# Weighing parts spaced by dense matmuls, a smaller memset and some value copies on VectorE, in an attention and token-MLP kernel

## The chip, the cores and the metric

The kernel runs on one core of a Trainium2 chip. Its time is device microseconds of one execution. A core has five engines that work side by side from their own instruction queues: TensorE (PE; its weight loads are listed as PEld), VectorE (DVE), ScalarE (ACT), GpSimd (POOL) and SyncE (SP, which issues the transfers here). An engine waits where an instruction needs another engine's result or a buffer that another engine still reads.

## What is computed

Two branches share one normalized input of 2048 tokens by 1024 features. Branch A is attention in 4 segments of 512 tokens, 32 heads of 32 columns, with a memory carried from segment to segment. Branch B is an MLP across tokens. Their sum and the input are the output.

```python
x  = A_x
xn = _layernorm(x)
return x + _A_ref(xn, wq, wk, wv, wo, beta) + _B_ref(xn, w1, b1, w2, b2)

# branch A, for each segment s, per head
logits = q_s @ k_s.T * scale + mask          # causal
a_dot  = softmax(logits) @ v_s
a_mem  = (phi(q_s) @ M) / (phi(q_s) @ z + 1e-06)
o      = g * a_mem + (1 - g) * a_dot
M, z   = M + phi(k_s).T @ v_s, z + sum(phi(k_s))
# at the end: o @ wo

# branch B
y = gelu(layernorm(xn).T @ w1 + b1) @ w2 + b2   # over tokens, transposed back
```

Here phi(t) is t + 1 for positive t and exp(t) otherwise.

## The kernel before

The program is written as one stream; a small framework class (`FW`) puts each operation on an engine and adds the waits that its reads and writes need. `FW.mm` (line 198) issues every matmul, so all matmuls have line 198 in the profile and are told apart by their tiles. PSUM has 8 banks of 128x512 fp32; the framework orders readers and writers by bank.

**First half.** Normalization, then branch B as two chains of block products (`products`, with seven products in place of eight for each 2x2 block of a pair of chunks). A result bank is added into fp32 `part` tiles on DVE (`add_bank`, line 690). While the last pair of the second chain runs, `before_attention` (from line 995) lays out the attention's tiles in memory that is no longer used, loads `wv` and `wo`, computes the gates (`gates`, lines 545 to 559, small DVE operations, the last of them a 128x32 copy at line 558), and sets the three value tiles `vA` to 1.0 on POOL (line 1024). A value tile is 128 x 4 x 16 x 33: 4 chunks of 128 tokens, 16 heads, 32 value columns and one column of ones. With that column, the product of probabilities and values also gives the softmax's row sum, and the memory product also gives z.

**Second half: `attention` (line 1350).** Work goes by units, u = 0 to 31: segment s = u // 8, and 4 heads at a time. A unit's own steps are these:

- `logits(u, step)`: scores of four heads in row tiles into banks 0 to 3, then one exp on ACT over 128x2048 into `pT` (line 1212), then the causal mask on the diagonal blocks on POOL (line 1216). Step 0 is key block 0; step 1 is key blocks 1 and 3; step 2, in even units alone, is key block 2 of two units. The three steps share banks 0 to 3, so each waits for the exp of the one before.
- `weigh(u - 1, part)`: the probabilities of the unit before, times `vA` (matmuls of 33 columns), and from segment 1 on phi(q) times the memory (132 columns). Parts 0 and 2 use bank 4, part 1 uses bank 5. Each part is copied by DVE into `ost` (line 1263). Part 2 also makes the memory update, which DVE adds into `MZ32` and writes masked to `MZbf` (lines 1269 to 1274).
- `combine(u - 1)`: reciprocals, gate, products and a sum on DVE, into `o_s` (lines 1284 to 1321); `phi_q`, `phi_k` (lines 1080 and 1082); two transposes by DMA; for some units one chunk of the next segment's input (`xn_scale`, line 986, and a transposing DMA). These steps are put on a list, `side`.

**Dense work.** Between these steps stand the projections, as jobs of 8 matmuls of 512 columns: `wo_job` for an output of an earlier segment, `v_job` for a chunk of values, `q_job` and `k_job` for the unit after next, in this order. `unit_jobs(u)` collects them: 24 matmuls in segment 0 and in some late units, 32 in most others. Jobs take turns on banks 6 and 7, so the job after next needs the bank that this one's result is copied from. The last matmul of a job is followed by its copy: ACT for q (line 1103) and, before the change, for every v (line 1139), DVE for k (line 1112) and for the output addition (`fin`, line 1154). `v_job(m, c)` makes chunk c of half-segment m; units 4(m-1) to 4(m-1)+3 hold the four chunks of m, and m = 0 stands ahead of unit 0.

`dense(n)` issues n of these matmuls. While `side` is not empty, it pops one of its steps after every third matmul. So the order within a unit is fixed by `cut(total, shares)`, which divides the unit's dense matmuls among the places between the steps:

- even units, shares (5, 1, 3, 15, 8) of 32: logits 0, 5, weigh 0 and 1, 1, weigh 2, 3, logits 1, 15, logits 2, 8;
- odd units, shares (7, 4, 1, 4, 16): 7, logits 0, 4, weigh 0 and 1, 1, weigh 2, 4, logits 1, 16.

With 24 matmuls the numbers are scaled and rounded: 4, 0, 3, 11, 6 and 5, 3, 1, 3, 12.

`tail` (line 1420) weighs the last unit and finishes the last 512 tokens' output.

Of the kernel before, what the change touches and what calls it, by code (L numbers as in the profile page):

```python
# [6 lines left out]
ACT = mybir.ActivationFunctionType  # L7
# [8 lines left out]
D_HEAD = 32  # L16
# [368 lines left out]
class _Kernel:  # L385
# [609 lines left out]
    def before_attention(self, p):  # L995
        fw = self.fw
        if p == 1:
            self.walk = _Walk(self.mem, self.G_AT, self.B_AT)
            for k in range(2):
                self.wq_ring.ensure(k)  # L1000
                self.wk_ring.ensure(k)
            self.gates()
        take = self.walk.take

        def many(name, n, shape, dtype, parts=1):
            tiles, res = [], []
            for k in range(n):
                t, r = take(f"{name}{k}", shape, dtype, parts)
                tiles.append(t)
                res.append(r if parts > 1 else r[0])  # L1010
            return tiles, res

        if p == 6:
            self.wv, self.R_wv = take("wv", [P, N_DCH, D_MODEL], BF16, 2)
            for bv in range(2):
                fw.dma(self.wv[:, :, bv * 512:(bv + 1) * 512],
                       self.A_wv[:, bv * 512:(bv + 1) * 512].rearrange("(dc p) j -> p dc j", p=P), writes=[self.R_wv[bv]])
            self.vA, self.R_vA = many("vA", 2, [P, 4, 16, VW], BF16, 4)
        elif p == 5:
            a, b = many("vA_", 1, [P, 4, 16, VW], BF16, 4)  # L1020
            self.vA += a
            self.R_vA += b
            for k in range(3):
                fw.op("pool", lambda e: e.memset(self.vA[k][:], 1.0), writes=self.R_vA[k])
            self.qT, self.R_qT = many("qT", 3, [P, SEG_L], BF16)
            self.kT, self.R_kT = many("kT", 3, [P, SEG_L], BF16)
            self.etmp, self.R_etmp = many("etmp", 4, [P, SEG_L], BF16)
            self.mtmp, self.R_mtmp = many("mtmp", 2, [P, SEG_L], BF16)
        elif p == 7:
            self.pqT, self.R_pqT = many("pqT", 3, [P, SEG_L], BF16)  # L1030
            self.pk, self.R_pk = many("pk", 2, [P, 4, P], BF16)
            self.ost, self.R_ost = many("ost", 2, [P, 32, VW], BF16, 3)
            self.o_s, self.R_os = many("o_s", 2, [P, 4, P], BF16)
            self.prod, (self.R_prod,) = take("prod", [P, 32, D_HEAD], BF16)
        elif p == 2:
            self.wo, (self.R_wo,) = take("wo", [P, N_GRP, D_MODEL], BF16)
            fw.dma(self.wo[:], self.A_wo.rearrange("(jc p) j -> p jc j", p=P), writes=[self.R_wo])
        elif p == 3:
            self.pT = take("pT", [P, 2, 4, PT_COLS], BF16)[0]
            base = self.mem.live.pop()  # L1040
            self.R_pu = [[Res(f"pu{b}{k}", dict(base[2][0].r)) for k in range(4)] for b in range(2)]
            self.R_pd = [[Res(f"pd{b}{k}", dict(base[2][0].r)) for k in range(4)] for b in range(2)]
            self.mem.live.append((base[0], base[1], [r for rows in self.R_pu + self.R_pd for r in rows]))
            self.xnT[1], self.R_xnT[1] = take("xnT1", [P, N_DCH, SEG_L], BF16, 4)
            w = _Walk(self.mem, self.B_AT, self.B_AT + self.STG_AT)
            self.MZ32, self.R_MZ32 = w.take("MZ32", [P, N_GRP, GW], F32, N_GRP)
            self.MZbf, self.R_MZbf = w.take("MZbf", [P, N_GRP, GW], BF16, N_GRP)
            self.diag, (self.R_diag,) = w.take("diag", [P, 4, VW], F32)
            self.oT, self.R_oT = [], []
            for k in range(2):  # L1050
                t, r = w.take(f"oT{k}", [P, N_GRP, SEG_L], BF16, N_GRP)
                self.oT.append(t)
                self.R_oT.append(r)
            w = _Walk(self.mem, self.B_AT + 88320, self.B_AT + 96512)
            self.fin, self.R_fin = [], []
            for k in range(4):
                t, r = w.take(f"fin{k}", [P, D_MODEL], BF16, 2)
                self.fin.append(t)
                self.R_fin.append(r)
            fw.op("dve", lambda e: e.memset(self.diag[:], 0.0), writes=[self.R_diag])  # L1060
            for r in range(4):
                fw.op("dve", lambda e: e.memset(self.diag[32 * r:32 * r + 32, r, :], 1.0),
                      reads=[self.R_diag], writes=[self.R_diag])
# [67 lines left out]
    def v_job(self, m, c):  # L1131
        s, bv, i = m // 2, m % 2, m % 3

        def mm(b, dc):
            self.fw.mm(self.bank(b), self.xnT[s % 2][:, dc, c * P:(c + 1) * P], self.wv[:, dc, bv * 512:(bv + 1) * 512],
                       start=(dc == 0), stop=(dc == 7))

        def end(b):
            self.fw.op("act", lambda e: e.activation(self.vA[i][:, c, :, 0:D_HEAD],  # L1139
                                                     self.bank(b).rearrange("p (h d) -> p h d", d=D_HEAD), ACT.Copy),  # L1140
                       reads=[self.R_bank[b]], writes=[self.R_vA[i][c]])

        return [0, None, lambda: [self.R_wv[bv], self.R_xnT[s % 2][c]], mm, end]

# [205 lines left out]
    def attention(self):  # L1350
        self.jobs, self.turn = deque(), 0
        self.side, self.since = deque(), 0
        self.exps, self.in_etmp = [], [None] * 4
        self.wo_plan = {}
        for s in range(N_SEG - 1):
            at = [N_GRP * s + 10 + n for n in range(8)] if s < 2 else [27, 28, 29, 30, 30, 31, 31, 31]
            for n, u in enumerate(at):
                self.wo_plan.setdefault(u, []).append((4 * s + n // 2, n % 2))
        self.jobs.extend([self.q_job(0), self.k_job(0)] + [self.v_job(0, c) for c in range(4)])
        self.dense(16)  # L1360
        self.late_exps()
        self.phi_k(0)
        self.k_transpose(0)
        self.jobs.extend([self.q_job(1), self.k_job(1)])
        self.dense(100)
        self.load_fin(0)
        self.load_fin(1)
        for u in range(N_UNIT):
            even = u % 2 == 0
            self.jobs.extend(self.unit_jobs(u))  # L1370
            total = 8 * len(self.jobs) - sum(j[0] for j in self.jobs)
            c = 4 * (u // N_GRP + 1) + u % N_GRP
            xn = u % N_GRP < 4 and c < N_TCH
            if xn:
                self.xn_load(c)
            cuts = self.cut(total, (5, 1, 3, 15, 8) if even else (7, 4, 1, 4, 16))
            if even:
                self.logits(u, 0)
            else:
                self.dense(cuts[0])  # L1380
                self.logits(u, 0)
            if u > 1:
                self.o_transpose_dma(u - 2)
            self.dense(cuts[0] if even else cuts[1])
            if u:
                self.weigh(u - 1, 0)
                self.weigh(u - 1, 1)
            self.dense(cuts[1] if even else cuts[2])
            if u:
                self.weigh(u - 1, 2)  # L1390
                steps = self.combine(u - 1)
                self.side.append(steps.pop(0))
            if N_GRP <= u:
                self.side.append(lambda: self.phi_q(u))
            if u:
                self.side.extend(steps)
            if u + 1 < N_UNIT:
                self.side.append(lambda: (self.phi_k(u + 1), self.k_transpose(u + 1)))
            if xn:
                self.side.append(lambda: (self.xn_scale(c), self.xn_transpose(c)))  # L1400
            self.dense(cuts[2] if even else cuts[3])
            self.logits(u, 1)
            if even:
                self.dense(cuts[3])
                self.logits(u, 2)
            self.dense(100)
            while self.side:
                self.side.popleft()()
        self.tail()
# [83 lines left out]
```

## Time and profile before

| | before |
|---|---|
| median of 3 runs | 671.02 us (670.72 to 673.8) |
| profiled execution | 676.49 us |
| its span in the trace | 674.8 us |
| TensorE busy | 648.7 us, 96% |
| VectorE busy | 424.5 us, 63% |
| ScalarE busy | 279.8 us, 41% |
| GpSimd busy | 148.4 us, 22% |
| mean granted TensorE clock | 0.995 |
| attention | from about 354 us to the end |

The profiled execution took 1.69 us more than its span; this lies before the first and after the last instruction of the trace. A row of the wait table reads: the engine, tile and line that waited, the engine, tile and line that released it, then us in total, the number of times and the longest one. A row of a timeline reads: start, duration, engine, line, operation, output tile <- input tiles, shape, count, and in brackets the idle time before it with what ended it. Times inside the trace count from the start of the span. In segment 0 (about 368 to 435 us) DVE is busy about half of the time and ACT about two thirds to four fifths; from 450 to 600 us DVE is busy over four fifths of the time.

### The profile page before, as it was taken

The numbers are of one execution on the slowest core, as the hardware profiler recorded it, in microseconds if no ns is written. First come the engines' busy times: TensorE is split into PE (matmuls) and PEld (weight loads), VectorE is DVE, ScalarE is ACT, GpSimd is POOL, SyncE is SP. The second block draws the span as 40 slices with busy tenths as digits, with TensorE's granted clock in tenths as the row PEclk, the third lists the DMA queues.
The fourth block names the chain that finished last, engine by engine and source line by source line (L and its number), as shares of the span: only waits on it lengthen the run. The fifth ranks groups of instructions, "written<-read, shape, count | busy, mean of one in ns | idle before, by whom it ended". The sixth has DMA issues, their size and how long they took to land.

```text
span 674.8 us, 11066 instructions
## 1 busy us (share of the span) xinstructions
PE 648.7 (96%) x4568; PEld 302.5 (45%) x4622; DVE 424.5 (63%) x813; ACT 279.8 (41%) x305; POOL 148.4 (22%) x181
## 2 busy tenths in 40 slices
PE   8999999999999999999989999989999999999988
PEld 3444444444444444444434444444444444444444
DVE  6975766656643344433632554578888888776795
ACT  7532322313200000000104777866767666667650
POOL 2500000000022022220430333333233233332340
PEclk9999999999999999999989999999999999999999
DMA  9704232422926755456555784457544774534324
GB/s 302 198 1 125 82 106 63 123 65 63 249 80 171 202 156 151 111 146 171 118 196 150 169 149 96 110 134 149 126 91 107 179 173 103 127 86 79 80 79 133
DMA packets 187243, 87.65 MB, mean 130 GB/s; under 512 B 116025, under 2 KB 174393, under 8 KB 187193
## 3 DMA queue, kind: packets, MB, share of 16 engines
q1 hardware_dynamic: 187048, 86.91, 50.9%
q8 instruction: 36, 0.59, 0.4%
q14 instruction: 15, 0.11, 0.1%
q10 hardware_dynamic: 144, 0.03, 0.0%
HBM read 67.13 MB, written 8.39 MB: 112 GB/s over the span
## 4 chain that ended last, share of the span: by engine, by line
PE 84%; DVE 10%; ACT 3%; issue 2%; DMA 1%; SPq 0%; DVEq 0%
PE ps_all L198 84%; DVE ost L1263 2%; ACT pT L1212 2%; DVE prod L1310 1%; DVE gate L558 1%; DVE mtmp L1080 1%; DMA xin<-in_A_x_dram 1%; DVE pqT L1082 1%; DVE fin L1440 1%; DVE kT L1112 1%; DVE mtmp L1082 1%; ACT vA L1139 0%; DVE fin L1154 0%; DVE srec L1305 0%; DVE o_s L1316 0%
## 5 line engine op out<-in xcount | busy, mean ns | idle before, releaser
L1212 ACT ACTIVATE pT<-ps_all 128x2048 bf16<-128x2048 f32 x80 | 150.1, 1876 | 63.9 <-PE ps_all L198 63.9
L1216 POOL TENSOR_SCALAR_AFFINE_SELECT pT<-pT 128x512 bf16<-128x512 bf16 x128 | 95.4, 762 | 212.4 <-ACT pT L1212 212.4
L690 DVE TENSOR_TENSOR part<-ps_all,part 128x512 f32<-128x512 f32 x76 | 57.3, 754 | 118.8 <-PE ps_all L198 117.9
L926 POOL TENSOR_TENSOR part<-part,stg 128x512 f32<-128x512 f32 x24 | 33.0, 1403 | 266.7 <-DVE part L690 266.7
L695 ACT ACTIVATE part<-ps_all 128x512 f32<-128x512 f32 x20 | 11.9, 597 | 149.0 <-PE ps_all L198 149.0
L742 ACT ACTIVATE g<-part,b1c 128x512 f16<-128x512 f32 x36 | 26.0, 722 | 98.8 <-DVE part L690 98.8
L1263 DVE CAST ost<-ps_all 128x396 bf16<-128x396 f32 (+2 forms) x96 | 42.9, 474 | 37.2 <-PE ps_all L198 37.2
L198 PE MATMUL ps_all<-xnT,wk 128*128 128x512 bf16 x251 | 60.6, 379 | 3.9 <-ACT vA L1139 3.1
L198 PE MATMUL ps_all<-wv,xnT 128*128 128x512 bf16 x238 | 62.9, 382 | 1.2 <-issue 0.8
L198 PE MATMUL ps_all<-wo,oT 128*128 128x512 bf16 (+2 forms) x249 | 59.6, 367 | 2.2 <-DVE fin L1154 0.9
L198 PE MATMUL ps_all<-xnT,wq 128*128 128x512 bf16 x248 | 60.2, 379 | 0.6 <-issue 0.5
L198 PE MATMUL ps_all<-g,sum 128*128 128x512 f16 x224 | 52.7, 388 | 2.6 <-DVE part L690 2.6
L198 PE MATMUL ps_all<-vA,pT 128*128 128x33 bf16 x1280 | 45.4, 178 | 9.0 <-DVE ost L1263 8.8
L198 PEld LDWEIGHTS ps_all<-vA,pT 128*128 128x128 bf16 x1280 | 42.0, 96 | 22.3 <-DVE ost L1263 12.9
L198 PE MATMUL ps_all<-g,w2s 128*128 128x512 f16 x224 | 51.0, 379 | 0.0
L198 PE MATMUL ps_all<-gT,sum 128*128 128x512 f16 x224 | 49.7, 379 | 0.0
L198 PE MATMUL ps_all<-h,sum 128*128 128x512 f16 x192 | 45.2, 379 | 0.0
L198 PE MATMUL ps_all<-h,w1s 128*128 128x512 f16 x192 | 44.9, 379 | 0.0
L198 PE MATMUL ps_all<-hT,sum 128*128 128x512 f16 x192 | 43.6, 379 | 0.0
L1310 DVE TENSOR_TENSOR prod<-ost,srec 128x512 bf16<-128x512 bf16 x48 | 40.2, 837 | 0.9
L1112 DVE CAST kT<-ps_all 128x512 bf16<-128x512 f32 x32 | 22.0, 687 | 26.9 <-PE ps_all L198 26.8
L198 PEld LDWEIGHTS ps_all<-xnT,wk 128*128 128x128 bf16 x256 | 23.4, 98 | 34.3 <-issue 9.0
(98 smaller groups left out, 815.8 us busy)
## 6 DMA issues: line engine op xcount, KB each, us to landing
w2s<-in_B_w_dram SPq DMA_DIRECT2D x8, 1792.0 KB, 8.6
w1s<-in_B_w_dram SPq DMA_DIRECT2D x12, 1024.0 KB, 5.6
wq<-in_A_wq_dram SPq DMA_DIRECT2D x32, 256.0 KB, 3.2
wk<-in_A_wk_dram SPq DMA_DIRECT2D x32, 256.0 KB, 3.5
stg<-in_A_x_dram SPq DMA_DIRECT2D x16, 256.0 KB, 3.0
xs<-in_A_x_dram SPq DMA_DIRECT2D x16, 256.0 KB, 3.6
out_dram<-stg SPq DMA_DIRECT2D x16, 256.0 KB, 3.0
fin<-out_dram SPq DMA_DIRECT2D x16, 256.0 KB, 3.2
```

What stands on the lines that cost most here:

```text
L198: ins = self.nc.tensor.matmul(*args, **kwargs)
L558: fw.op("dve", lambda e: e.tensor_copy(self.gate[:, :, 1, :], gv), reads=[self.R_gcol, self.R_gate], writes=[self.R_gate])
L690: self.fw.op("dve", lambda e: e.tensor_tensor(self.tmp[dst][:], self.bank(b), self.tmp[src][:], op=ALU.add), reads=[self.R_bank[b], self.R ...
L695: self.fw.op("act", lambda e: e.activation(self.tmp[dst][:], self.bank(b), ACT.Copy), reads=[self.R_bank[b]], writes=[self.R_tmp[dst]])
L742: self.fw.op("act", lambda e: e.activation(self.gB[f % 2][half][:, f // 2, :], src, ACT.Gelu_apprx_tanh, bias=self.b1c[:, f:f + 1], scale= ...
L926: fw.op("pool", lambda e: e.tensor_tensor(self.tmp[t][:], self.tmp[t][:], self.stg[k][:, 512 * half:512 * half + 512], op=ALU.add), reads= ...
L1082: fw.op("dve", lambda e: e.scalar_tensor_tensor(dst, src, 1.0, mt[:], op0=ALU.add, op1=ALU.max), reads=[R_src, self.R_mtmp[k]], writes=[R_ ...
L1112: fw.op("dve", lambda e: e.tensor_copy(self.kT[k][:], self.bank(b)), reads=[self.R_bank[b]], writes=[self.R_kT[k]])
L1212: fw.op("act", lambda e: e.activation(dst, src, ACT.Exp, scale=SCALE), reads=self.R_bank[0:4], writes=[R[v % 2][kb] for v, kb, _ in blocks ...
L1216: fw.op("pool", lambda e: e.affine_select(d, d, pattern=[[0, 4], [1, P]], compare_op=ALU.is_ge, fill=0.0, base=0, channel_multiplier=-1), ...
L1263: fw.op("dve", lambda e: e.tensor_copy(dst, src), reads=[self.R_bank[b]], writes=[self.R_ost[o][part]])
L1310: fw.op("dve", lambda e: e.tensor_tensor(self.prod[:, n, :], ost[:, n, 0:D_HEAD], rec[:, n].unsqueeze(2).to_broadcast([P, 16, D_HEAD]), op ...
```

## The change

Three edits. In `before_attention` the memset of each value tile touches the column of ones alone (64 elements a partition in place of 2112). In `v_job`, the copies of half-segments m = 1 and m = 2, which are made in units 0 to 7, go to VectorE; all others stay on ScalarE. In `attention` the cuts have new shares, and the three weighing parts no longer follow one another closely: part 1 has a place of its own, with 2 of 32 dense matmuls on each side, and part 2 is followed by 2 rather than 3 or 4 before logits 1.

With 32 dense matmuls the new orders are:

- even: logits 0, 4, weigh 0, 2, weigh 1, 2, weigh 2, 2, logits 1, 14, logits 2, 8;
- odd: 7, logits 0, 3, weigh 0, 2, weigh 1, 2, weigh 2, 2, logits 1, 16.

With 24: 3, 1, 2, 2, 10, 6 in the dense places of even units, and 5, 3, 1, 1, 2, 12 in those of odd ones.

```diff
@@ before_attention
             for k in range(3):
-                fw.op("pool", lambda e: e.memset(self.vA[k][:], 1.0), writes=self.R_vA[k])
+                fw.op("pool", lambda e: e.memset(self.vA[k][:, :, :, D_HEAD:], 1.0), writes=self.R_vA[k])
@@ v_job
         def end(b):
-            self.fw.op("act", lambda e: e.activation(self.vA[i][:, c, :, 0:D_HEAD],
-                                                     self.bank(b).rearrange("p (h d) -> p h d", d=D_HEAD), ACT.Copy),
-                       reads=[self.R_bank[b]], writes=[self.R_vA[i][c]])
+            dst, src = self.vA[i][:, c, :, 0:D_HEAD], self.bank(b).rearrange("p (h d) -> p h d", d=D_HEAD)
+            if m in (1, 2):
+                self.fw.op("dve", lambda e: e.tensor_copy(dst, src), reads=[self.R_bank[b]], writes=[self.R_vA[i][c]])
+            else:
+                self.fw.op("act", lambda e: e.activation(dst, src, ACT.Copy), reads=[self.R_bank[b]],
+                           writes=[self.R_vA[i][c]])
@@ attention
-            cuts = self.cut(total, (5, 1, 3, 15, 8) if even else (7, 4, 1, 4, 16))
-            if even:
-                self.logits(u, 0)
-            else:
-                self.dense(cuts[0])
-                self.logits(u, 0)
+            cuts = self.cut(total, (0, 4, 2, 2, 2, 14, 8) if even else (7, 3, 2, 2, 2, 16))
+            self.dense(cuts[0])
+            self.logits(u, 0)
             if u > 1:
                 self.o_transpose_dma(u - 2)
-            self.dense(cuts[0] if even else cuts[1])
+            self.dense(cuts[1])
             if u:
                 self.weigh(u - 1, 0)
+            self.dense(cuts[2])
+            if u:
                 self.weigh(u - 1, 1)
-            self.dense(cuts[1] if even else cuts[2])
+            self.dense(cuts[3])
             if u:
                 self.weigh(u - 1, 2)
                 steps = self.combine(u - 1)
...
-            self.dense(cuts[2] if even else cuts[3])
+            self.dense(cuts[4])
             self.logits(u, 1)
             if even:
-                self.dense(cuts[3])
+                self.dense(cuts[5])
                 self.logits(u, 2)
```

## The prediction

> **What bounds the kernel now.** First the shares and the wait table (who waited for whom: total us, times, longest), then the timeline around each wait.
>
> ```profile
> PE 648.7 (96%) x4568; PEld 302.5 (45%) x4622; DVE 424.5 (63%) x813; ACT 279.8 (41%) x305; POOL 148.4 (22%) x181
> ...
> PEld ps_all L198 <- DVE ost L1263: 12.9, 27, 2.1
> ...
> PE ps_all L198 <- DVE ost L1263: 8.8, 24, 1.7
> ...
> PE ps_all L198 <- ACT vA L1139: 3.1, 6, 0.5
> ...
> PE ps_all L198 <- DVE part L690: 2.6, 1, 2.6
> ```
>
> TensorE is the bound: it stands idle 26 of 674.8 us, and each edit aims at one of the last three rows. A matmul's modelled end hides part of a wait, so I price waits from start to start: a 512-column matmul starts 0.216 us after the one before (28 of them, 331.26 to about 337.32), a 33-column one after 0.0256, a 132-column one after 0.055, a logits step takes 0.33. 54 matmul records are missing (4,568 against 4,622 weight loads); most sit right behind a wait, so a 0.40 gap with a matmul of the code missing in it counts as 0.18.
>
> The largest single loss is at the start of the attention (timelines of POOL, DVE and PE, then windows: PE, PEld, DVE, ACT, POOL busy, clock, DMA):
>
> ```profile
> 334.51 5.45 POOL L1024 MEMSET vA<- 128x2112 bf16 x3 [9.93 <-PE ps_all L198]
> ...
> 334.45 5.54 DVE L558 COPY gate<-gcol 128x32 f32<-128x32 f32 x1
> 334.54 5.45 DVE L690 TENSOR_TENSOR part<-ps_all,part 128x512 f32<-128x512 f32 x1
> ...
> 340.07 4.88 PE L198 MATMUL ps_all<-g,sum 128*128 128x512 f16 x14 [2.60 <-DVE part L690]
> ...
> 340.00:342.00 2.00, 1.93 (x5) 0.70 (x6) 0.00 (x0) 0.00 (x0) 0.00 (x0) 0.55 1.07 349
> 342.00:344.00 2.00, 2.00 (x7) 0.76 (x6) 0.00 (x0) 0.00 (x0) 0.00 (x0) 0.60 0.11 33
> ```
>
> A 128x32 copy takes 5.54 us where the like of it at L556 takes 0.18; it ends with the third memset. The sum behind it (L690) is what product 7 waits for. Then TensorE runs at 0.55 to 0.60 of its clock until 344.
>
> Inside the attention, two repeating waits (a unit of segment 0):
>
> ```profile
> 385.09 0.56 PE L198 MATMUL ps_all<-vA,pT 128*128 128x33 bf16 x16 [0.31 <-DVE ost L1263]
> ...
> 389.43 0.59 PE L198 MATMUL ps_all<-xnT,wk 128*128 128x512 bf16 x2 [0.51 <-ACT vA L1139]
> ...
> 386.92 1.88 ACT L1212 ACTIVATE pT<-ps_all 128x2048 bf16<-128x2048 f32 x1 [1.26 <-PE ps_all L198]
> 388.70 0.59 ACT L1139 ACTIVATE vA<-ps_all 128x512 bf16<-128x512 f32 x1
> ```
>
> Weighing part 2 reuses bank 4, so it waits for the ost copy of part 0; a key projection reuses the bank of the value job, whose copy stands behind a 1.88 us exp on ACT. The third kind is a late DVE (unit 10):
>
> ```profile
> 450.70 0.69 DVE L1082 SCALAR_TENSOR_TENSOR mtmp<-kT,mtmp 128x512 bf16<-128x512 bf16 x1
> 451.31 0.86 DVE L986 TENSOR_SCALAR xs<-xs,ln_mv,ln_rs 128x1024 bf16<-128x1024 bf16 x1
> 452.09 1.03 DVE L1263 CAST ost<-ps_all 128x396 bf16<-128x396 f32 x2
> ...
> 452.70 0.62 PE L198 MATMUL ps_all<-vA,pT 128*128 128x33 bf16 x16 [1.72 <-DVE ost L1263]
> ```
>
> DVE has worked without a break from part 2's copy of the unit before (444.84) to this copy.
>
> [...] the kT copy, 128x512 from PSUM, took 0.69 us (0.61 where another follows), and that is my price for a value copy on VectorE.
>
> **1. The memsets.** Each 128x2112 memset (1.858 us) becomes 128x64, strided. Nearest rows: 0.112 us for 128x16 fp32, 0.204 for 128x128; I take 0.16 (up to 0.5 if the stride costs), so three end near 335.0 instead of 339.95. The gate copy and the 0.75 us sum end by 336, before TensorE wants the bank at 337.32: 1.3 us of cover, and the upper price still fits. Gone: the stall, 340.07 − 337.32 = 2.75, and the slow clock, 14 matmuls in 4.72 us (340.07 to 344.79) instead of 3.03 = 1.69. Sum 4.4. Nothing else is late there: after 340 the chain of waits holds TensorE alone until 368.
>
> **2. The value copies.** In even units with 24 dense matmuls the old cuts put logits 1 after dense 7, the value job ends at 8, and its copy queues behind exp 1: 0.67 us in each of units 0, 2, 4, 6, 8 and 26 (start to start; the table shows 0.5 each), together 4.05. The new cuts put logits 1 after dense 8, so even where the copy stays on ACT (8 and 26) it stands ahead of that exp. In units 0 to 7 it goes to DVE; in an even unit it follows part 2's copy, two MZ steps and the scales, is done some 2.1 us after part 2 ends, and is wanted 2.5 us after it. I leave 0.1 each for units 0, 8 and 26 (there exp 1 starts later and logits 2 waits). Gain 3.7. In an odd unit the value job ends right before part 0, so the copy stands ahead of part 0's ost copy: that is counted in 3. DVE is busy 15 of 30 us here; the eight copies (4.9 us) fit.
>
> **3. The weighing.** From the end of part 0 to the end of its ost copy seen by TensorE takes 0.81 us with a 128x396 copy (0.57 and the latencies around it), about 0.77 in segment 0. Now TensorE fills this with part 1 (0.31 or 0.41) and one dense or none. Old waits by unit, missing records allowed for: units 2, 4, 6, 8: 0.46 each; 1, 3, 5, 7: 0.16 each; fifteen units from 9 to 30: 0.18 each; 26 and 28: 0.40; 29 and 31: 0.43; late DVE in 10, 12, 18, 20: 1.87, 0.62, 0.61, 0.60. Sum 10.5.
> After, part 1 and four dense (two to three where a unit has 24) cover 1.27 or about 0.95 us, so waits set by the copy's own latency go. What stays:
> - Odd units 1, 3, 5, 7: value copy starts 0.19 after the job ends, ost copy follows at 0.80, ends 1.24; part 2 is wanted at 1.05. 0.24 each, 0.96 together: slightly worse than now.
> - Units where DVE is late. Its chain runs from part 2 of the odd unit to part 0's copy in the even one, and TensorE's work from part 2 to part 2 is 4+16+5+1 = 26 dense before and 2+16+4+2+2 = 26 after. Nothing is gained: 12, 18, 20 stay (1.83), and 14, 16, 22, whose 0.18 is also at the end of an unbroken DVE chain (0.54). Unit 10 has 22 dense instead of 21: 1.65, probably with its slow clock.
> - 29 and 31, behind a fin addition of 0.69: 0.22 each.
> Left 5.4, gain 5.1. Of this 0.4 is given back: in unit 30 logits 2 waits for exp 1 anyway, and after 31 the end is a DVE chain. Gain 4.7.
> The splits cost no start: from 512 to 33 columns there is no gap where no wait stands (a dense start at 483.72, the weighing's at 483.94). On SP, loads of wq or wk move ahead of transposes of pk or xnT by one place, and the transpose now waits for that load's slot; pk is read two units later, xnT two units or more.
>
> **Sum** in the profiled execution: 4.4 + 3.7 + 4.7 = 12.8 of 674.8, to a span of 662.0; with the 1.69 around it 663.7 against 676.5. The median of the plain runs is 5.5 below the profiled one, so some stall, perhaps the slow clock of 1.69, may be missing in them: gain 11.1 to 12.8, I take 12.0: 659.0.
>
> **Rivals.**
> - The waits for ost stay as a whole, because DVE, not the bank, is late once TensorE runs closer to it. For: DVE busy 42 of 50 us from 450 to 550. Against: in segments 0 and 3 it has idle time before the copy (0.90 before the one at 384.52). Then steps 1 and 2 alone pay, 8.1 less the 0.8 that I took off for the plain runs: 663.7.
> - The wait of unit 10 and its slow clock (about 1.7) fall as well, and the late units shift: 4 more, 655. For: POOL's masks move against DVE's chain, which holds 0.3 to 0.4 us stretches (prod 1.01, o_s 0.74 against 0.43). Against: the same 26 dense.
> - Slower: that shift goes the other way. Logits 1 now comes two dense (0.43 us) sooner after part 2, so the masks (0.76 us each, two in a row) fall on other DVE operations between part 2 and the next unit's part 0 copy. One microsecond more in each of eight late units, and the half clock behind four of them (1.7 each), is 15; it decides from about 12 us, 1.5 per unit, and gives 674.5. Against: the masks already block that chain for some 0.75 us per unit.
> - The edits cancel: no change, 670.
>
> **Chances.** Forecast 0.60, first rival 0.15, second 0.13, no change 0.05, slower 0.07. A change within 0.5% (3.4 us) can't be told from none here. Faster 0.88. The range, 655 to 667, holds the forecast with a memset or copy at its upper price, the first rival with a slow-clock window on top (1.7 to 2), and the near half of the second.
>
> **What would show it.** The gate copy back near 0.2 us and no slow clock at 340. No wait of TensorE for vA in even units. Waits for ost only in units 1 to 7 (odd, about 0.2) and in the even units of segments 1 and 2, with unit 10 the longest. The forecast is wrong if the ost total stays near 12.9, if TensorE waits for pT between logits 1 and 2, or if new slow-clock windows appear.

## The result and the profile after

| | before | after | ratio, 95% interval |
|---|---|---|---|
| median, first comparison | 671.75 us | 661.78 us | 0.9848 (0.9816 to 0.988) |
| median, second comparison | 671.91 us | 662.65 us | 0.9848 (0.9826 to 0.987) |
| profiled execution | 676.49 us | 660.95 us | |
| its span | 674.8 us | 659.2 us | |

The kernel is 1.5% faster: 10.0 us, where 12.0 were forecast. From here on, "plain time" is the median of the times of whole executions, with those of the kernel before that ran beside them as the comparison. The two profiled executions lie 15.5 us apart, so they differ by more than the kernels do. Much of this study is about that gap.

The shares of the engines and two rows of the wait table of the kernel after:

```profile
PE 648.0 (98%) x4622; PEld 302.0 (46%) x4622; DVE 425.3 (65%) x821; ACT 276.0 (42%) x297; POOL 148.5 (23%) x181
...
PEld ps_all L198 <- DVE ost L1266: 8.8, 14, 2.1
...
PE ps_all L198 <- DVE ost L1266: 3.1, 6, 1.6
```

The rows of TensorE waiting for vA and for part are gone, and the row for ost is down from 8.8 us in 24 waits to 3.1 in 6. The six waits are in units 10, 12, 18, 20, 30 and 31; those of units 1, 3, 5 and 7 are too short for the table (below). One sign of being wrong did appear: in unit 30 TensorE waits 0.37 us for pT between logits 1 and 2, where it had waited 0.15 before. All 4,622 matmuls have a record here, which fits the reading of the short gaps before as missing records. The start of the attention, by POOL, DVE and PE:

```profile
334.17 0.66 POOL L1024 MEMSET vA<- 128x64 bf16 x2 [9.93 <-PE ps_all L198]
337.19 0.38 POOL L1024 MEMSET vA<- 128x64 bf16 x1 [2.36 <-PE ps_all L198]
...
334.11 0.76 DVE L558 COPY gate<-gcol 128x32 f32<-128x32 f32 x1
334.20 0.68 DVE L690 TENSOR_TENSOR part<-ps_all,part 128x512 f32<-128x512 f32 x1
...
336.96 3.19 PE L198 MATMUL ps_all<-g,sum 128*128 128x512 f16 x14
339.99 3.19 PE L198 MATMUL ps_all<-g,w2s 128*128 128x512 f16 x14
```

Two strided 128x64 memsets take 0.66 us and a single one 0.38 (I took 0.16 each, at most 0.5). The gate copy takes 0.76 us, not the forecast 0.2: it ends just after the second memset. That costs nothing, since product 7 starts without a wait, and its 14 matmuls take 3.03 us instead of 4.72.

Logits 0 stands at or near the start of every unit, so the time from one logits 0 to the next gives a unit's length. How much shorter each unit is after than before, in these first two profiles (worked out from starts rounded to 0.01 us):

```text
unit   0    1     2     3     4     5     6     7     8     9    10
us   0.69 -0.09  1.14 -0.08  1.13 -0.08  1.14 -0.09  1.15  0.20 1.60
unit 11..25, odd 0.19 to 0.21, even 0.15 to 0.24
unit  26   27    28    29    30
us   1.09  0.20  0.41  0.21 -0.50
```

From the start of unit 0 to the start of unit 31 this is 11.0 us. Ahead of unit 0 lie another 4.8: 0.3 from a start that differs, 4.5 from the memset. The tail is 0.3 longer.

### The profile page after: what moved, and what is told of

It is laid out like the page before. It is cut to its first block, busy times and chain, and to the rows that moved or that the text cites. A ratio compares the mean times of both kernels' runs of the same rounds, so it can differ in the third digit from the quotient of the medians.

```text
span 659.2 us, 11114 instructions
## 1 busy us (share of the span) xinstructions
PE 648.0 (98%) x4622; PEld 302.0 (46%) x4622; DVE 425.3 (65%) x821; ACT 276.0 (42%) x297; POOL 148.5 (23%) x181
## 4 chain that ended last, share of the span: by engine, by line
PE 87%; DVE 9%; DMA 2%; issue 1%; ACT 0%; DVEq 0%
PE ps_all L198 87%; DVE prod L1313 2%; DMA w2s<-in_B_w_dram 1%; DVE ost L1266 1%; DVE pqT L1082 1%; DVE fin L1157 1%; DVE fin L1442 1%; DVE o_s L1319 0%; DVE sum L649 0%; DVE kT L1112 0%; DVE vA L1141 0%; DMA xin<-in_A_x_dram 0%; DVE mtmp L1080 0%; DVE srec L1308 0%; DVE mtmp L1082 0%
## 5 line engine op out<-in xcount | busy, mean ns | idle before, releaser
L1219 POOL TENSOR_SCALAR_AFFINE_SELECT pT<-pT 128x512 bf16<-128x512 bf16 x128 | 99.8, 797 | 197.2 <-ACT pT L1215 197.2
L690 DVE TENSOR_TENSOR part<-ps_all,part 128x512 f32<-128x512 f32 x76 | 52.5, 691 | 119.1 <-PE ps_all L198 118.2
L198 PE MATMUL ps_all<-wv,xnT 128*128 128x512 bf16 x256 | 69.1, 379 | 0.0
L198 PE MATMUL ps_all<-wo,oT 128*128 128x512 bf16 (+2 forms) x272 | 65.8, 367 | 1.2 <-DVE fin L1157 1.2
L198 PE MATMUL ps_all<-xnT,wq 128*128 128x512 bf16 x256 | 63.6, 380 | 0.0
L1266 DVE CAST ost<-ps_all 128x396 bf16<-128x396 f32 (+2 forms) x96 | 44.3, 475 | 25.7 <-PE ps_all L198 24.3
L198 PEld LDWEIGHTS ps_all<-vA,pT 128*128 128x128 bf16 x1280 | 45.0, 96 | 24.3 <-DVE ost L1266 8.8
L198 PE MATMUL ps_all<-vA,pT 128*128 128x33 bf16 x1280 | 48.6, 178 | 3.6 <-DVE ost L1266 3.1
L198 PE MATMUL ps_all<-g,sum 128*128 128x512 f16 x224 | 51.0, 379 | 0.0
L198 PEld LDWEIGHTS ps_all<-wo,oT 128*128 128x128 bf16 x272 | 23.4, 97 | 26.0 <-issue 5.4
```

Of the source, the lines that this page charges most:

```text
L198: ins = self.nc.tensor.matmul(*args, **kwargs)
L690: self.fw.op("dve", lambda e: e.tensor_tensor(self.tmp[dst][:], self.bank(b), self.tmp[src][:], op=ALU.add), reads=[self.R_bank[b], self.R ...
L1219: fw.op("pool", lambda e: e.affine_select(d, d, pattern=[[0, 4], [1, P]], compare_op=ALU.is_ge, fill=0.0, base=0, channel_multiplier=-1), ...
L1266: fw.op("dve", lambda e: e.tensor_copy(dst, src), reads=[self.R_bank[b]], writes=[self.R_ost[o][part]])
```

## The experiments

Theory: three mechanisms that add up. A GpSimd memset holds the gate copy on VectorE (step 1; 5.54 us in the first profile, ending with the third memset); the place of logits 1 decides the waits for vA (step 2); part 2 waits for the latency of part 0's copy, except where VectorE's chain is late (step 3). The main rivals: the engine of the value copies is what counts, and the first profile shows an execution that is not the usual one.

### The memset alone

```diff
-                fw.op("pool", lambda e: e.memset(self.vA[k][:], 1.0), writes=self.R_vA[k])
+                fw.op("pool", lambda e: e.memset(self.vA[k][:, :, :, D_HEAD:], 1.0), writes=self.R_vA[k])
```

> The kernel before with the small memset alone. Theory [...]: product 7 starts about 2.7 us sooner and the slow clock after it is gone, so the next landmark (first g,w2s matmul after it) comes 4.4 us sooner counted from the start of gT,sum; plain time 2.7 to 4.5 us less, about 667.8. Nothing else moves: waits for ost and vA as before, the long wait of unit 10 with them. Rival (the wait was for something else that merely ended with the memsets): gate copy still long, under 0.5 us gained.

In the trace all came as expected: the stretch from the first gT,sum matmul to the first g,w2s matmul after it took 9.06 us against 13.53, that is 4.47 less, and every unit of the attention has its old length within 0.01 us but unit 10 (0.15 longer). The plain time hardly moved: 671.8 against 672.36, ratio 0.9986 (0.9976 to 0.9997), about 0.9 us by the ratio. So the loss that the first profile shows is not in most executions.

### The cuts alone

```diff
-            cuts = self.cut(total, (5, 1, 3, 15, 8) if even else (7, 4, 1, 4, 16))
+            cuts = self.cut(total, (0, 4, 2, 2, 2, 14, 8) if even else (7, 3, 2, 2, 2, 16))
```

with parts 1 and 2 in their new places; memset and value copies as before.

> The kernel before with the new cuts alone; value copies stay on ScalarE, memset full. Theory (the place of logits 1 decides the vA waits, not the engine of the copy): all six waits for vA gone, even units 2 to 8 and 26 each about 1.1 us shorter, and odd units 1, 3, 5, 7 about 0.16 shorter, where the whole change had them 0.08 longer; memset stall and slow clock stay. Plain time 8 to 10 us less, about 662.5. Rival (the copies on VectorE are what frees the bank): vA waits stay in units 0 to 6, gain under 6 us.

660.86 us, ratio 0.9824 (0.9808 to 0.984): 11.5 less, above the expected 8 to 10. No TensorE wait for vA is left: the new place of logits 1 is enough to remove them, with every copy still on ScalarE. Even units 2 to 8 and unit 26 are 1.1 us shorter, units 1, 3, 5, 7 are 0.17 to 0.19 shorter. One expectation fell: the memset stall did not appear, although the memsets are full (views of DVE and POOL):

```profile
336.15 1.95 DVE L558 COPY gate<-gcol 128x32 f32<-128x32 f32 x1
336.24 1.86 DVE L690 TENSOR_TENSOR part<-ps_all,part 128x512 f32<-128x512 f32 x1
...
336.20 5.48 POOL L1024 MEMSET vA<- 128x2112 bf16 x3 [9.94 <-PE ps_all L198]
```

The copy was held for one memset and got in before the second. At 1.95 us it ends 0.9 us ahead of TensorE's need (the first matmul of product 7 starts at 339.00).

### The value copies on VectorE alone

```diff
-            self.fw.op("act", ...
+            if m in (1, 2):
+                self.fw.op("dve", lambda e: e.tensor_copy(dst, src), ...
```

> The kernel before with the value copies of half-segments 1 and 2 on VectorE alone. Theory: waits for vA gone in units 0, 2, 4, 6 (0.67 each, 2.7), left in 8 and 26; in odd units 1, 3, 5, 7 the copy stands ahead of part 0's ost copy and makes part 2 wait about 0.3 to 0.4 longer each (1.2 to 1.6). Net 1 to 1.5 us less. Rival (VectorE has room for the copies, they cost nothing): 2.7 us less.

670.11 us, ratio 0.9965 (0.9951 to 0.9979): 2.3 less. Units 0, 2, 4, 6 are 0.67 to 0.76 shorter, units 1, 3, 5, 7 0.29 to 0.31 longer. By unit lengths the sum is 1.6 (unit 10 left out); the theory holds in both signs. The plain gain lies nearer to the rival's 2.7, but the unit lengths speak against the rival: the copies do cost time in odd units. Unit 8, whose copy stays on ScalarE, gains only 0.08.

### The change with all value copies on ScalarE

```diff
-            if m in (1, 2):
+            if m in ():
```

> The changed kernel with all value copies back on ScalarE. Theory: the copies on VectorE cost 0.24 us in each of units 1, 3, 5, 7 and bring about 0.1 at most in the even ones, so this is 0.5 to 1.0 us faster than the changed kernel in the profile's units, no wait for ost in units 1 to 8. Rival (the copies carry a part of the gain): vA waits come back in units 0 to 6, about 2.7 us slower than the changed kernel.

659.82 us, ratio 0.9818 (0.9802 to 0.9834). In the profiles, from unit 0 to unit 31, it is 1.1 us faster than the changed kernel, 0.26 of it in each of units 1, 3, 5, 7 and nothing lost in the even ones; the intervals of the two plain times overlap. In the changed kernel unit 3 looks like this (DVE, then PE):

```profile
387.41 0.69 DVE L1141 CAST vA<-ps_all 128x512 bf16<-128x512 f32 x1 [1.47 <-PE ps_all L198]
388.02 0.62 DVE L1266 CAST ost<-ps_all 128x264 bf16<-128x264 f32 x2
...
388.03 0.38 PE L198 MATMUL ps_all<-xnT,wq 128*128 128x512 bf16 x1
388.50 0.57 PE L198 MATMUL ps_all<-vA,pT 128*128 128x33 bf16 x16
```

Part 2 (the last row) should follow the dense matmul after 0.22 us, at 388.25; it starts 0.25 later, when part 0's ost copy, pushed back by the value copy, is done. By unit lengths, once the cuts are changed, this edit only costs.

### The kernel before, profiled again

No edit.

> The kernel before, profiled a second time. After four looks the 5.54 us gate copy has been seen in one of three profiles with the full memsets (1.95 us in the two others, where VectorE got in after the first memset). Theory now (which of the two happens is decided anew in each execution): 1.95 us and no stall of product 7, or 5.54 us with it; the clock stays low for some 3 us behind unit 10 in either case. Rival (the order of the kernel before always gives 5.54): 5.54 again.

DVE and POOL:

```profile
333.98 1.95 DVE L558 COPY gate<-gcol 128x32 f32<-128x32 f32 x1
...
334.03 5.48 POOL L1024 MEMSET vA<- 128x2112 bf16 x3 [9.93 <-PE ps_all L198]
```

The gate copy took 1.95 us and product 7 did not wait. The two profiled executions of this one kernel took 676.49 and 671.82 us; of these 4.67 us, 4.47 lie in the stretch around product 7 (13.53 against 9.06 us). So the stall, with the slow clock behind it, is what set the first profile so far above the median. In four profiles with the three full memsets and the copy on VectorE, 5.54 was seen once. An estimate from this: a loss of 2.75 (the stall alone) to 4.4 us in one of four executions is 0.7 to 1.1 us on average, which fits the 0.9 of the memset alone.

The wait of unit 10 is the same in every profile with the old cuts (1.72 us); the slow clock behind it came here too (next experiment).

### The gate copy on ScalarE

```diff
-        fw.op("dve", lambda e: e.tensor_copy(self.gate[:, :, 1, :], gv),
+        fw.op("act", lambda e: e.activation(self.gate[:, :, 1, :], gv, ACT.Copy),
```

> The kernel before with only the last gate copy moved from VectorE to ScalarE; memsets stay full. Theory ([...] the sum behind it reads PSUM and was merely queued): the sum takes 0.7 us while the memsets run, product 7 starts without a wait. Rival (any VectorE operation is held by a GpSimd memset): the sum takes 2 us or more.

DVE and POOL:

```profile
336.26 0.69 DVE L690 TENSOR_TENSOR part<-ps_all,part 128x512 f32<-128x512 f32 x1
...
336.28 5.45 POOL L1024 MEMSET vA<- 128x2112 bf16 x3 [9.94 <-PE ps_all L198]
```

The sum, which reads a PSUM bank, runs at its usual 0.69 us while POOL's first memset runs, and the three memsets keep their 5.45 us, so neither held the other. What was held in the profiles of the kernel before is the copy, which goes from SBUF to SBUF (5.54 us in the first, 1.95 when profiled again); whether that is why was not tested. The sum merely stood behind it in the queue: in the first profile of the kernel before and with the cuts alone it ends together with the copy, not its own 0.69 us later. This is the one run here that separates the two.

This profile also separates the wait of unit 10 from the slow clock. First this kernel, the wait and the window around it, then the same two lines of the kernel before profiled again; in a window's row the third figure from the end is the clock, 1.00 being full speed:

```profile
450.02 0.57 PE L198 MATMUL ps_all<-vA,pT 128*128 128x33 bf16 x16 [1.72 <-DVE ost L1263]
...
440.00:460.00 20.00, 18.26 (x189) 8.72 (x187) 16.97 (x36) 13.64 (x14) 6.77 (x8) 1.00 0.58 128
```

```profile
447.77 0.57 PE L198 MATMUL ps_all<-vA,pT 128*128 128x33 bf16 x16 [1.72 <-DVE ost L1263]
...
440.00:460.00 20.00, 18.28 (x162) 7.98 (x161) 16.25 (x35) 12.21 (x12) 5.81 (x7) 0.91 0.56 127
```

The same wait of 1.72 us is followed by the slow clock in one execution and not in another: of six profiles with the old cuts, four have it there. Unit 10 is 1.4 us shorter without it. In the first profile of the kernel before, both slow stretches last 3.4 us at a clock of 0.50: the one behind the wait of unit 10 from 452.84 to 456.24 us, and the one behind the stall, which ends like this:

```profile
340.20:343.60 3.40, 3.40 (x9) 1.18 (x8) 0.00 (x0) 0.00 (x0) 0.00 (x0) 0.50 0.63 203
343.60:345.00 1.40, 1.40 (x7) 0.59 (x6) 0.01 (x1) 0.00 (x0) 0.00 (x0) 1.00 0.00 0
```

Half of 3.4 us is a quarter of a percent of the span, so, as an estimate, a mean clock of 0.997 fits one such stretch and 0.995 two; that profile reports 0.995 and has this one and one behind unit 10. Of 70 executions of the kernel before, 19 report a mean clock of 1.000 (median 670.84 us), 48 of 0.997 (672.36) and 3 of 0.995 (673.88): a slow stretch goes with some 1.5 us. Not each of them lies behind unit 10: in some profiles one lies in the first 20 us (with the cuts alone the mean clock there is 0.91). Of 8 executions of the changed kernel 6 report 1.000.

### Half the spacing

```diff
-            if m in (1, 2):
+            if m in ():
-            cuts = self.cut(total, (0, 4, 2, 2, 2, 14, 8) if even else (7, 3, 2, 2, 2, 16))
+            cuts = self.cut(total, (0, 4, 1, 1, 4, 14, 8) if even else (7, 3, 1, 1, 4, 16))
```

> The changed kernel with value copies on ScalarE (as in e4_after_act_copies) and shares of one dense matmul on each side of part 1 instead of two, the two freed ones put behind part 2. Theory (part 2 waits for the latency of part 0's copy, 0.81 us from its end, and 0.41 + 2 x 0.216 covers that): units with 32 dense have no more wait than with four; units with 24 get back their old counts (odd: one dense, 0.16 each in 1, 3, 5, 7, 9; even: one dense, 0.24 each in 2, 4, 6, 8, 26, 28). About 2 us slower than e4_after_act_copies. Rival (each part has a wait of its own that needs two dense): 0.2 more in each of sixteen further units, 5 us slower.

664.57 us, ratio 0.988 (0.9862 to 0.9899); from unit 0 to unit 31 it is 3.5 us slower than with two dense matmuls on each side, between theory (2) and rival (5). Units 1 to 9 lose 0.18 to 0.25 each and units 26 and 28 0.20 as expected, and odd units with 32 dense matmuls lose nothing, as the theory has it. But the even ones from 12 to 22 lose 0.16 to 0.17 each, which it had not (nor 0.20 in unit 10, 0.22 in unit 29 and a gain of 0.28 in unit 30). DVE and POOL from unit 13 to unit 14 show most of the reason. Spacing one, then the changed kernel:

```profile
476.71 0.43 DVE L1266 CAST ost<-ps_all 128x264 bf16<-128x264 f32 x1 [0.33 <-PE ps_all L198]
...
479.25 1.41 DVE L1313 TENSOR_TENSOR prod<-ost,srec 128x512 bf16<-128x512 bf16 x2
480.69 0.74 DVE L1319 TENSOR_TENSOR o_s<-prod 128x512 bf16<-128x512 bf16 x1
481.35 0.72 DVE L1080 TENSOR_SCALAR mtmp<-etmp 128x512 bf16<-128x512 bf16 x1
...
483.31 1.03 DVE L1266 CAST ost<-ps_all 128x396 bf16<-128x396 f32 x2
...
480.01 1.92 POOL L1219 TENSOR_SCALAR_AFFINE_SELECT pT<-pT 128x512 bf16<-128x512 bf16 x2 [3.35 <-ACT pT L1215]
```

```profile
474.38 0.43 DVE L1266 CAST ost<-ps_all 128x264 bf16<-128x264 f32 x1 [0.55 <-PE ps_all L198]
...
476.92 1.72 DVE L1313 TENSOR_TENSOR prod<-ost,srec 128x512 bf16<-128x512 bf16 x2
478.68 0.74 DVE L1319 TENSOR_TENSOR o_s<-prod 128x512 bf16<-128x512 bf16 x1
479.34 0.28 DVE L1080 TENSOR_SCALAR mtmp<-etmp 128x512 bf16<-128x512 bf16 x1
...
480.87 1.03 DVE L1266 CAST ost<-ps_all 128x396 bf16<-128x396 f32 x2
...
477.25 1.90 POOL L1219 TENSOR_SCALAR_AFFINE_SELECT pT<-pT 128x512 bf16<-128x512 bf16 x2 [3.35 <-ACT pT L1215]
```

From part 2's copy to the next unit's part 0 copy, VectorE takes 6.60 us with spacing one, as in the kernel before (486.02 to 492.63, 6.61), and 6.49 with spacing two: 0.11 of the 0.17. Another 0.05 lies behind logits 1, ahead of the q job, and was not looked into. The same operations run, but logits 1 follows part 2 by two dense matmuls instead of four, so POOL's masks fall on other operations: 0.44 us on mtmp before, 0.31 on prod after. That the masks cause these extra times is inferred: masks run at those moments in each trace, and no run took them away.

### k copies of odd units on ScalarE

```diff
-            fw.op("dve", lambda e: e.tensor_copy(self.kT[k][:], self.bank(b)),
-                  reads=[self.R_bank[b]], writes=[self.R_kT[k]])
+            if u % 2 and u > 8:
+                fw.op("act", lambda e: e.activation(self.kT[k][:], self.bank(b), ACT.Copy),
+                      reads=[self.R_bank[b]], writes=[self.R_kT[k]])
+            else:
+                fw.op("dve", lambda e: e.tensor_copy(self.kT[k][:], self.bank(b)),
+                      reads=[self.R_bank[b]], writes=[self.R_kT[k]])
```

on top of the change with all value copies on ScalarE. As written, the edit also moves the copy of unit 9's k, made at the end of unit 7; no unit length shows it.

> As e4_after_act_copies, with the copy of k for odd units from 11 on (made in odd units 9 to 29) on ScalarE instead of VectorE. Theory (the waits left in units 10, 12, 18, 20 end an unbroken VectorE chain, so 0.6 us less in the chain is 0.6 us less wait): unit 10 waits 1.1 instead of 1.7, units 12, 18, 20 not at all; 2.0 us faster than e4_after_act_copies, and no slow clock behind unit 10. Rival (the chain then waits for something else, exp or masks): under 0.5 us.

Against that kernel unit 10 is 0.58 us shorter, units 12, 18 and 20 0.50 to 0.51, unit 30 0.48, all others within 0.05. Unit 10's wait (PE):

```profile
443.20 0.57 PE L198 MATMUL ps_all<-vA,pT 128*128 128x33 bf16 x16 [0.98 <-DVE ost L1270]
```

In the kernel with the k copy on VectorE it is 1.56. Taking 0.6 us out of an unbroken VectorE chain took as much out of the wait at its end (0.58 in unit 10), where there was that much. From unit 0 to unit 31 that makes 2.7 us, where the theory had 2.0 and the rival under 0.5; unit 30 was not in the theory. The plain time is 658.69 us, ratio 0.9796 (0.978 to 0.9813): the lowest of this study, and in the profiles faster than the changed kernel by 3.8 us from unit 0 to unit 31.

### One memset for two tiles

```diff
-            self.vA, self.R_vA = many("vA", 2, [P, 4, 16, VW], BF16, 4)
+            both, R = take("vA01", [P, 2, 4, 16, VW], BF16, 8)
+            self.vA01, self.vA, self.R_vA = both, [both[:, 0], both[:, 1]], [R[0:4], R[4:8]]
-            for k in range(3):
-                fw.op("pool", lambda e: e.memset(self.vA[k][:], 1.0), writes=self.R_vA[k])
+            fw.op("pool", lambda e: e.memset(self.vA01[:], 1.0), writes=self.R_vA[0] + self.R_vA[1])
+            fw.op("pool", lambda e: e.memset(self.vA[2][:], 1.0), writes=self.R_vA[2])
```

> The kernel before with the first two value tiles side by side and set by one memset of 128x4224 instead of two of 128x2112; the third as before. Theory ([...] product 7 waits once the sum ends after its 6.05 us of cover): the gate copy takes 3.8 us in every profile, unless the third memset holds it too (5.6 us); product 7 waits 0.9 to 1.1 us (or 2.7). Plain time 0.5 to 1.5 us more than before; if the wait also brings the slow clock of 1.7, up to 3. Rival (what is lost is only what shows in the profile taken first, nothing in plain runs): no difference.

DVE, POOL and PE:

```profile
334.09 3.71 DVE L558 COPY gate<-gcol 128x32 f32<-128x32 f32 x1
...
334.15 3.62 POOL L1024 MEMSET vA<- 128x4224 bf16 x1 [9.93 <-PE ps_all L198]
...
337.88 3.19 PE L198 MATMUL ps_all<-g,sum 128*128 128x512 f16 x14 [0.78 <-DVE part L690]
```

The copy ends 0.04 us after the end of a memset: with one of double length it takes 3.71 us, where it took 1.95 behind a single one of 128x2112. So it was held for the memset's whole length here (3.62 us, and 1.86 for one of 128x2112 in the first profile of the kernel before). It did not always get in after the first: with 128x2112 it ended after the first or the third, and in all six profiles with 128x64 after the second (0.76 us, two memsets in 0.66). The plain time rises to 674.69 from 671.91, ratio 1.0039 (1.0024 to 1.0055), that is 2.6 us: more than the 0.5 to 1.5 expected for the wait alone, and within the 3 expected if slow clock comes with it. The profile, one of the fastest of 22 executions (671.34, where they lie between 671.1 and 677.92), shows a wait of 0.8 to 0.9 us and a clock of 1.00; 7 of the 22 report a clock of 0.995, against 2 of 27 of the kernel before beside them. Where the slower ones lose their time is not shown.

### The changed kernel again

No edit.

> The changed kernel again, for a second profile and more plain runs. Theory: unit lengths of the attention as in its first profile within 0.05 us each, start of the span different by up to 2 us; unit 10 waits 1.6 to 1.7; plain ratio to the kernel before 0.983 to 0.986. Rival (the first profile was a lucky execution in the attention too): unit lengths differ by more.

Every unit has the length of the first profile within 0.01 us; only the start of the span is 2.1 us later, with a slow clock (0.91) in the first 20 us. So within a kernel the attention repeated to 0.01 us in the profiles, unit 10 with its slow clock apart; what varied between executions is the start, which memset the copy got in after, and the slow clock.

## Why the prediction was right, and where its terms were off

The direction and the range were right, the size was 2.0 us too large. In part that is luck: step 1 was priced far too high for plain time, and the steps in the attention brought about 1 us more than forecast. Between the two profiles, which it worked from, the gap was 15.5 us against 12.8 worked out. By its steps:

1. **The memsets.** Mechanism right: a memset held the copy for its whole length (1.95 and 3.71 us behind one of 128x2112 and of 128x4224), the sum merely stood behind it, 4.47 us gone in the trace against 4.4 worked out. That the slow clock would go with the stall was my assumption; both went. That the copy would be back near 0.2 us was wrong, at no cost. The size was wrong for plain time: the step took a loss of 2.7 to 4.4 us from one execution, and it was there in one of four profiles. Alone it brought 0.9 us (0.2 to 1.6). The text did doubt the slow clock in plain runs, since the median lay 5.5 us below the profiled run; it did not doubt the stall, which the same gap called into question. This is the term that was mis-sized.
2. **The value copies.** Six waits of 0.67 are gone, and the 0.1 set aside in units 0, 8 and 26 were not needed: 4.0 instead of 3.7. The cuts alone do it; the move to VectorE adds nothing in the even units and costs about 1.1 us in the odd ones.
3. **The weighing.** Units 1, 3, 5, 7: 0.24 left was worked out, 0.24 to 0.25 measured. Units set by the copy's latency lost their waits. "Nothing is gained" in the units where VectorE is late was wrong: 12, 14, 16, 18, 20 and 22 gained 0.16 to 0.20 each. In the one looked at, 0.11 of it is a shorter VectorE chain, with the masks on other operations; that the masks are the cause is inferred, and the text named this only in its rivals. Unit 30 lost 0.5 instead of coming out even: its part 0 copy stands behind a k copy there, and with that copy on ScalarE it came out even (0.02).
4. **Unit 10.** 0.2 was forecast, 1.6 was in the profile. The wait itself went from 1.87 to 1.72, start to start; the other 1.4 is the slow clock. Here the second rival was right in part: the slow clock did become rarer. None of the six profiles with changed cuts (the one with spacing one among them) has it behind unit 10, and 5 of 26 executions of these kernels report a clock below 1.000, against 89 of 128 with the old cuts. But it had the clock recover because the wait falls, and with spacing one the wait is still 1.72 us. What keeps the clock up is not shown.

The terms against plain time, as an estimate: the profile of the kernel before with the gate copy on ScalarE, with neither stall nor slow clock in the attention, is 9.6 us longer from unit 0 to unit 31 than the changed kernel (steps 2 and 3 had 8.4); the tail gives 0.2 back; the slow clock, reported below 1.000 in 51 of 70 executions before and 2 of 8 after at some 1.5 us, adds 0.7. That is 10.1, and 11.0 with the 0.9 that the memset brought alone; measured were 10.0, and 9.3 in the second comparison. Both intervals take in 11.0, so how much the memset adds within the whole change is not settled.

The first rival (the waits for ost stay as a whole) fell; the slower one did as well: the chain that the masks fall on got 0.1 us shorter, not longer, in the late unit looked at.

## What to carry to other kernels

Before a stall from one profile is priced, it is worth asking whether it repeats: a profiled time well above the median says that some loss in it is not usual, and a loss that hangs on which of two engines gets in first (here a copy of 1.95 or 5.54 us) is a candidate. A second profile of the same kernel would have told here. Waits that come from an order of work repeated to 0.01 us here, and most could be forecast to 0.2. An operation moved to a less busy engine is still queued there: here what stood right behind it decided (part 2 of unit 3 started 0.25 us later), and by unit lengths a version that only changed the order was 1.1 us faster than the one that also moved copies.

## What the runs showed of the hardware beyond what I expected

With three GpSimd memsets of 128x2112 in a row, a waiting VectorE copy got in after the first in three of four profiles and after the third in one; with those of 128x64 it got in after the second in six of six. What decides was not found: in the four of these profiles that are printed (one of them in the prediction) the copy's recorded start lies 0.05 to 0.06 us ahead of the first memset's, and the copy still waited. An idle stretch of TensorE of 1.72 us was followed by a slow clock in four of the six profiles with the old cuts and not in the other two (a mean clock of 0.91 or 0.92 against 1.00 over 20 to 22 us around it; in the first profile of the kernel before, 3.4 us at 0.50), and the mean clock that executions report (1.000, 0.997, 0.995) sorts their times by some 1.5 us a step. What decides there was not found either, and no run tested it.
